# RWKV attention and an MLP mixer on one core: own-step sums from turned products, staggered loads, and a new order of batches zero and one

## The chip, the cores and the metric

The kernel runs on one core of a Trainium2 chip. The metric is the device time of one execution in microseconds (us).

## The reference

Inputs in f32: r, k, v of shape (4, 8, 768, 48), that is batch, head, step, dimension; w and u of shape (8, 48); four weight matrices of the mixer. The attention is a recurrence over the 768 steps, with a decay w and a bonus u for the step's own key:

```python
for t in range(S):
    kt, vt, rt = (k[:, :, t], v[:, :, t], r[:, :, t])
    cur = np.einsum('bhd,bhe->bhde', u[None] * kt, vt)
    y[:, :, t] = np.einsum('bhd,bhde->bhe', rt, state + cur)
    state = w[None, :, :, None] * state + np.einsum('bhd,bhe->bhde', kt, vt)
```

Its output, as x of shape (4, 768, 384), goes through a mixer, first over the steps (tokens), then over the 384 channels:

```python
h = np.maximum(xt @ w_tok1, 0.0) @ w_tok2      # xt: x with steps last
u = x + h.transpose(0, 2, 1)
h2 = np.maximum(u @ w_ch1, 0.0) @ w_ch2
return u + h2
```

Here w_tok1 is 768x256, w_tok2 256x768, w_ch1 384x1536, w_ch2 1536x384.

## The kernel before

**Units.** A batch's 768 steps are cut into 6 chunks of 128 (T), so there are 24 units (b, c). In a unit the recurrence becomes matrix products over 128 steps: k is multiplied by a decay that grows with the step (`wn`) and r by one that shrinks (`wp`), so that scores of decayed k and r, masked to earlier steps, carry the decay between two steps. A state of 4 head pairs goes from unit to unit and is rescaled every third one (`wGm`).

**Stages of a unit.** `stage_p` (L266) makes the decayed k (`kp`) and, in batches 1 to 3, the decayed r (`rp`) and `ku` = k times u, all on POOL but for some `kp` in batch 0. `stage_a` (L288) turns both with transposes on TensorE (PE), copies them out of PSUM as `rk` on ScalarE (ACT), and makes a bf16 copy `vb` of v. `stage_b` (L325) makes the scores `at_ps` on PE and masks them on VectorE (DVE) into `AT`, two instructions of 512 columns. `stage_c` (L351) makes y on PE from the state and from `AT` times v, adds the unit to the state, and on DVE adds the own-step part `yd` into `x_b`.

**The own step.** The step's own term needs, for each step and head, the sum over d of r*u*k, called `adg`. In batches 1 to 3 DVE multiplies `ku` by r (`rku`) and reduces it. In batch 0 POOL makes `m` = k*r, PE turns it in f32, ACT copies it out, and PE multiplies it by `u_blk`, a block matrix of u by head (`ad_ps`). In both, POOL then multiplies v by `adg` into `yd` (`own_step`, L321). In batch 0 r is turned undecayed in f32 (`trr`), from padded tiles (`rpads`), and multiplied after the turn by a turned decay `wpT`.

**Mixer.** `token_mix` (L399) has three parts: `hidden` (token matmuls and relu), `back` (second matmul and the sum `u_sb`) and the turn of `u_sb` into `uT`: on PE for batch 0 (`turn`), by DMA transposes for the others. The channel mixer is `up` (L442: a tile of 128 of the 1536 hidden channels in `z_ps`, relu on ACT into `zr`; 12 tiles for each half `sg` of a batch) and `down` (L453: 12 matmuls for a chunk's output, then the sum `osb` on DVE and a store).

**Order.** A wrapper (`InOrder`) keeps every engine's instructions in the order in which the program issues them. Batch 0 runs in nine slots (L483), in each of which `slot` calls stage_c, b, a and p of four successive units. `keep_warm` puts idle matmuls between. Then the token mixing of batch 0, the first ups with three turns between them, and lists of ups and downs into which `merge` (L520) puts slots of the later batches at given times on a cost scale (an up 0.5, a down 2.0, a slot 1.4).

**Loads.** SP's queue issues the loads of k, r, v, unit by unit (`load_unit`, L82), 192 KB each. POOL's queue issues the weights, which are cast to bf16 on the way: wtok1 in slot 4, wtok2 in slot 5, the first half of wch1 in slot 6, its second half and wch2 in slot 7 (`WEIGHTS_AT`, L247). The first load of batch 1 waits for x_b of the last unit of batch 0 (`after[1, 0] = done[0, C - 1]`, L508), and with it all loads behind it.

All instructions are recorded through the wrapper's line 68, so the profile's rows are told apart by tile names.

Of the kernel before, what the change touches and what calls it, by code (L numbers as in the profile page):

```python
# [11 lines left out]
f32 = mybir.dt.float32  # L12
# [10 lines left out]
def kernel(  # L23
# [51 lines left out]

    loaded = {}
# [3 lines left out]
    rpads = [const.tile([128, H, P], f32, name=f"rpad{c}") for c in range(C)]  # L80

    def load_unit(b, c):  # L82
        tiles = []
        for nm, src in (("kt", k), ("rt", r), ("vt", v)):
            if b == 0 and nm == "rt":
                t = rpads[c]
                dst = t[:, :, 0:D]
            else:
                t = lpool.tile([128, dm], f32, name=nm)
                dst = h3(t)  # L90
            ins = sp.dma_start(dst, src[b, :, ts(c, T), :].rearrange("h s d -> s h d"))
            if (b, c) in after and nm == "kt":
                tc.add_manual_dep(ins.ins, after[b, c].ins.name,
                                  mybir.DependencyInfo(mybir.DependencyClass.Sync,
                                                       mybir.DependencyReason.DATA),
                                  reason="weights first")
            tiles.append(t)
        loaded[b, c] = tiles

    u_bc = const.tile([128, dm], f32, name="u_bc")
    ud = const.tile([128, 3], f32, name="ud")
    w_row = const.tile([1, dm], f32, name="w_row")
    u_row = const.tile([1, dm], f32, name="u_row")
    w_pairs = const.tile([HP, 2, P], f32, name="w_pairs")
    u_rows = const.tile([3, 128], f32, name="u_rows")
    ones = const.tile([1, 128], f32, name="ones")
    act.dma_start(w_row, w.rearrange("h d -> (h d)").unsqueeze(0))  # L110
    dve.memset(w_pairs, 1.0)
    dve.memset(ones, 1.0)
    act.dma_start(w_pairs[:, :, 0:D], w.rearrange("(a q) d -> a q d", q=2))
    act.preload_act_table_set("natural_log_exp_and_others")
    load_unit(0, 0)
    load_unit(0, 1)
    act.dma_start(u_rows, u.rearrange("h d -> (h d)").rearrange("(j p) -> j p", p=128))
    act.dma_start(u_row, u.rearrange("h d -> (h d)").unsqueeze(0))
# [13 lines left out]
    iota_i = const.tile([128, 2 * G], i32, name="iota_i")  # L132
    for g in range(G):
        pool.iota(iota_i[:, g:g + 1], pattern=[[0, 1]], base=g * T - MID, channel_multiplier=1)
        pool.iota(iota_i[:, G + g:G + g + 1], pattern=[[0, 1]], base=MID - 1 - g * T,
                  channel_multiplier=-1)
    iota = const.tile([128, 2 * G], f32, name="iota")
    dve.tensor_copy(iota, iota_i)
    steps_i = const.tile([128, G * T], i32, name="steps_i")
    pool.iota(steps_i, pattern=[[1, G * T]], base=-MID, channel_multiplier=0)  # L140
    steps = const.tile([128, G * T], f32, name="steps")
    dve.tensor_copy(steps, steps_i)
# [4 lines left out]
    for t in rpads[:2]:  # L147
        dve.memset(t[:, :, D:P], 0.0)
# [7 lines left out]
    heads = const.tile([128, 3, H], f32, name="heads")  # L156
    pool.memset(heads, 1.0)
    pool.affine_select(out=heads, in_=heads, compare_op=ALU.is_ge, fill=0.0, base=0,
                       pattern=[[128, 3], [-D, H]], channel_multiplier=1)
    pool.affine_select(out=heads, in_=heads, compare_op=ALU.is_ge, fill=0.0, base=D - 1,  # L160
                       pattern=[[-128, 3], [D, H]], channel_multiplier=-1)

    NB = 3
    rps = []; kps = []; S0s = []
    for i in range(NB):
        kp_i = const.tile([128, H, P], bf16, name=f"kp{i}")
        dve.memset(kp_i, 0.0)
        kps.append(kp_i)

    keep_warm(WARM[0] - 6)  # L170
    w_bc = psM.tile([128, dm], f32, name="w_bc", tag="m")
    pe.matmul(w_bc, ones, w_row, start=True, stop=True)
    wd = psM.tile([128, HP], f32, name="wd", tag="m")
    pe.transpose(wd, w_pairs.rearrange("a q d -> a (q d)"), ident_f[0:HP, 0:HP])
    ud_ps = psM.tile([128, 3], f32, name="ud_ps", tag="m")
    pe.transpose(ud_ps, u_rows, ident_f[0:3, 0:3])
    keep_warm(3)
    lnw = const.tile([128, dm], f32, name="lnw")
    act.activation(lnw, w_bc, Ln)
    wn = const.tile([128, G, dm], f32, name="wn")  # L180
    wp = const.tile([128, G, dm], f32, name="wp")
    lnwd = const.tile([128, HP], f32, name="lnwd")
    wpT = const.tile([128, G, HP, T], f32, name="wpT")

    def decay_k(g):
        act.activation(wn[:, g, :], lnw, Exp, scale=iota[:, G + g:G + g + 1])

    def decay_r(g):
        act.activation(wp[:, g, :], lnw, Exp, scale=iota[:, g:g + 1])

    def decay_rT(g):
        if g == 0:
            for a in range(HP):
                act.activation(wpT[:, g, a, :], steps[:, ts(g, T)], Exp, scale=lnwd[:, a:a + 1])
        else:
            act.activation(wpT[:, g], powers[g - 1], Exp)

    powers = [const.tile([128, HP, T], f32, name=f"powers{g}") for g in range(1, G)]

    def exponents(g):  # L200
        pool.tensor_mul(powers[g - 1], steps[:, ts(g, T)].unsqueeze(1).to_broadcast([128, HP, T]),
                        lnwd.unsqueeze(2).to_broadcast([128, HP, T]))

    decay_k(0)
    act.activation(lnwd, wd, Ln)
    act.copy(ud, ud_ps)
    wG = const.tile([128, HP], f32, name="wG")
    decay_rT(0)
    u_blk = const.tile([128, 3, H], f32, name="u_blk")


    for i in range(2):
        S_i = const.tile([128, HP, 2, D], bf16, name=f"S0_{i}")
        S0s.append(S_i)
    bm = const.tile([128, HP, 2, D], f32, name="bm")
    wGm = const.tile([128, HP, 2, D], f32, name="wGm")


    dve.memset(bm, 0.0)
    for q in range(2):  # L220
        dve.memset(bm[q * P:q * P + D, :, q, :], 1.0)
    for t in rpads[2:]:
        dve.memset(t[:, :, D:P], 0.0)
    for t in S0s:
        dve.memset(t, 0.0)

    def constants_1():
        pool.tensor_mul(u_blk, heads, ud.unsqueeze(2).to_broadcast([128, 3, H]))

    def constants_2():  # L230
        act.activation(wG, lnwd, Exp, scale=float(G * T))
        pool.tensor_mul(wGm, bm, wG.unsqueeze(2).unsqueeze(3).to_broadcast([128, HP, 2, D]))

    def constants_3():

        for i in range(NB):
            rp_i = const.tile([128, H, P], bf16, name=f"rp{i}")
            dve.memset(rp_i, 0.0)
            rps.append(rp_i)

# [4 lines left out]
    wch2 = wts.tile([128, NJ, dm], bf16, name="wch2")  # L245

    WEIGHTS_AT = {4: (0,), 5: (1,), 6: (2,), 7: (3, 4)}  # L247

    def load_weights(which):
        half = ds(0, dch // 2), ds(dch // 2, dch // 2)  # L250
        parts = [(wtok1, moe_w_tok1), (wtok2, moe_w_tok2), (wch1[0], moe_w_ch1[:, half[0]]),
                 (wch1[1], moe_w_ch1[:, half[1]]), (wch2, moe_w_ch2)]
        for i in which:
            t, src = parts[i]
            pool.dma_start(t, src.rearrange("(c p) k -> p c k", p=128))
# [3 lines left out]

    live = {}  # L260
    kv = [None]
    count = [0]

    BY_POOL = (3, 5)

    def stage_p(b, c):  # L266

        g = c % G
        kt, rt, vt = loaded.pop((b, c))
        i = count[0] % NB  # L270
        count[0] += 1
        kp = kps[i]
        vb = apool.tile([128, dm], bf16, name="vb", bufs=4)
        L = live[b, c] = dict(kp=kp, vb=vb, rt=rt, vt=vt)
        (dve if b == 0 and c not in BY_POOL else pool).tensor_mul(kp[:, :, 0:D], h3(kt), h3(wn[:, g, :]))
        if b == 0:
            L["m"] = apool.tile([128, dm], f32, name="m", bufs=2)
            pool.tensor_mul(h3(L["m"]), h3(kt), rt[:, :, 0:D])
        if b > 0:
            L["rp"] = rps[i]  # L280
            pool.tensor_mul(L["rp"][:, :, 0:D], h3(rt), h3(wp[:, g, :]))
            L["ku"] = apool.tile([128, dm], f32, name="ku", bufs=2)
            pool.tensor_mul(L["ku"], kt, u_bc)

    def pair(t, a):
        return t[:, 2 * a:2 * a + 2, :].rearrange("p q d -> p (q d)")

    def stage_a(b, c):  # L288

        L = live[b, c]  # L290
        rk = L["rk"] = apool.tile([128, 2, HP, T], bf16, name="rk")
        if b == 0:

            trk = psM.tile([128, HP, T], bf16, name="trk", tag="m")
            trr = psM.tile([128, HP, T], f32, name="trr", tag="m")
            for a in range(HP):
                pe.transpose(trk[:, a, :], pair(L["kp"], a), ident)
            act.copy(rk[:, 0], trk)
            for a in range(HP):
                pe.transpose(trr[:, a, :], pair(L["rt"], a), ident_f)  # L300
            dve.tensor_mul(rk[:, 1], trr, wpT[:, c % G])
            mT_ps = psM.tile([128, 3, T], f32, name="mT_ps", tag="m")
            for j in range(3):
                pe.transpose(mT_ps[:, j, :], L["m"][:, ts(j, 128)], ident_f)
# [302 lines left out]
```

## Time and profile before

| | |
|---|---|
| median of 3 runs | 185.45 us (185.41 to 185.52) |
| profiled execution | 184.74 us |
| its span | 182.8 us |
| TensorE clock granted | 1.00 |
| DMA | 24.05 MB, mean 132 GB/s |
| instructions: PE / DVE / ACT / POOL | 1507 / 194 / 219 / 113 |

The span runs from the first to the last recorded instruction of the profiled execution. A row of a group gives what is written from what (`out<-in`), shapes, count, busy time, the mean of one in nanoseconds, and the idle time of the engine just before, with the releaser. Rows of a timeline give start and length in us. Matmuls are pipelined: the mean of one is longer than the time from one to the next.

### The profile page before, as it was taken

What the parts mean: (1) busy time and instruction counts of PE and PEld (TensorE: products, weight loads), DVE (VectorE), ACT (ScalarE), POOL (GpSimd) and SP (SyncE); (2) the same over time, 40 slices, a digit from 0 to 9 for tenths busy, and PEclk for the clock granted to TensorE, in tenths of its full rate; (3) what the DMA queues carried; (4) which work ended last, traced back from release to release, by engine and by line L of the source; (5) the groups of instructions that cost most, each with busy time, mean ns of one, the idle gap of its engine ahead of it and who ended that gap; (6) DMA issues with size and microseconds to landing.
All of it is one profiled execution on the core that took longest, in us unless ns stands there. A gap on an engine that the chain in (4) does not pass through costs nothing.

```text
span 182.8 us, 4000 instructions
## 1 busy us (share of the span) xinstructions
PE 166.5 (91%) x1507; PEld 107.7 (59%) x1507; DVE 105.2 (58%) x194; ACT 100.1 (55%) x219; POOL 94.3 (52%) x113
## 2 busy tenths in 40 slices
PE   6999888894997997898999998999999999999992
PEld 2578675462664665556666665756665565666660
DVE  7385877620498999856659868996531061121121
ACT  2777465585867553506949747564545344445500
POOL 5767796004999999925499997981100000000000
PEclk9999999999999999999999999999999999999999
DMA  6999799999999999334799999633001034211212
GB/s 112 182 179 173 139 113 184 190 184 206 183 195 189 192 198 224 108 66 110 127 217 191 184 213 203 131 64 108 24 24 65 20 93 82 87 43 46 83 47 86
DMA packets 89272, 24.05 MB, mean 132 GB/s; under 512 B 82849, under 2 KB 89254, under 8 KB 89254
## 3 DMA queue, kind: packets, MB, share of 16 engines
q1 hardware_dynamic: 85824, 20.65, 62.4%
q0 software_dynamic: 3408, 3.15, 11.5%
q8 instruction: 12, 0.20, 0.5%
q14 instruction: 6, 0.05, 0.1%
q10 hardware_dynamic: 22, 0.01, 0.0%
HBM read 20.45 MB, written 4.72 MB: 138 GB/s over the span
## 4 chain that ended last, share of the span: by engine, by line
PE 53%; POOL 14%; DMA 13%; SPq 7%; DVE 6%; issue 3%; ACT 2%; POOLq 0%; DVEq 0%; ACTq 0%
PE h_ps L68 25%; PE z_ps L68 18%; DMA rt<-in_r_dram 7%; SPq L68 7%; POOL rp L68 4%; DMA rpad<-in_r_dram 3%; POOL yd L68 3%; POOL kp L68 3%; POOL ku L68 3%; PE tr_ps L68 3%; DMA kt<-in_k_dram 2%; PE hT_ps L68 2%; PE y_ps L68 2%; DVE AT L68 2%; PE at_ps L68 2%
## 5 line engine op out<-in xcount | busy, mean ns | idle before, releaser
L68 ACT ACTIVATE zr<-z_ps 128x384 bf16<-128x384 f32 x96 | 43.9, 496 | 31.1 <-PE z_ps L68 31.1
L68 PE MATMUL z_ps<-uT,wch 128*128 128x384 bf16 x288 | 52.1, 326 | 1.7 <-DVE osb L68 0.7
L68 PE MATMUL h_ps<-wch,zr 128*128 128x384 bf16 x288 | 50.4, 326 | 0.3 <-ACT zr L68 0.2
L68 DVE TENSOR_TENSOR osb<-u_sb,h_ps 128x384 f32<-128x384 bf16 x24 | 13.3, 553 | 46.0 <-PE h_ps L68 43.8
L68 PEld LDWEIGHTS <-zr 128*128 128x128 bf16 x288 | 28.0, 98 | 19.1 <-issue 1.1
L68 PEld LDWEIGHTS <-wch 128*128 128x128 bf16 x288 | 27.3, 98 | 19.5 <-issue 3.5
L68 POOL TENSOR_TENSOR kp<-kt,wn 128x384 bf16<-128x384 f32 x20 | 22.9, 1146 | 19.2 <-PE z_ps L68 10.9
L68 DVE TENSOR_TENSOR AT<-at_ps,mask 128x512 bf16<-128x512 f32 x48 | 30.7, 681 | 1.4 <-PE at_ps L68 1.4
L68 ACT COPY rk<-tr_ps 128x1024 bf16<-128x1024 bf16 x18 | 18.2, 1012 | 18.3 <-PE tr_ps L68 17.4
L68 POOL TENSOR_TENSOR yd<-vb,adg 128x384 f32<-128x384 bf16 x24 | 20.0, 834 | 7.3 <-DVE adg L68 6.7
L68 DVE TENSOR_TENSOR rku<-ku,rt 128x384 f32<-128x384 f32 x18 | 16.1, 892 | 9.7 <-POOL ku L68 9.6
L68 POOL TENSOR_TENSOR rp<-rt,wp 128x384 bf16<-128x384 f32 x18 | 18.6, 1031 | 2.1 <-DMA rt<-in_r_dram 2.1
L68 POOL TENSOR_TENSOR ku<-kt,u_bc 128x384 f32<-128x384 f32 x18 | 19.3, 1072 | 0.0
L68 DVE TENSOR_TENSOR x_b<-y_ps,yd 128x384 bf16<-128x384 f32 x24 | 13.3, 554 | 9.2 <-PE y_ps L68 5.4
L68 PEld LDWEIGHTS <-rk 48*128 48x128 bf16 (+1 forms) x272 | 11.3, 95 | 5.3 <-issue 2.0
L68 ACT CAST S<-kv_ps 48x192 bf16<-48x192 f32 x32 | 9.9, 310 | 7.4 <-PE kv_ps L68 7.1
L68 PEld LDWEIGHTS <-kp 128*128 128x128 bf16 x176 | 11.2, 101 | 4.4 <-POOL kp L68 0.9
L68 PEld LDWEIGHTS <-wtok 128*128 128x128 bf16 x96 | 9.1, 98 | 7.6 <-issue 2.4
L68 DVE TENSOR_TENSOR u_sb<-x_b,hT_ps 128x384 bf16<-128x384 bf16 x24 | 11.8, 548 | 2.3 <-PE hT_ps L68 2.3
L68 ACT CAST vb<-vt 128x384 bf16<-128x384 f32 x24 | 12.4, 515 | 0.0
L68 PE MATMUL tr_ps<-ident,rp 128*128 128x128 bf16 x72 | 7.0, 220 | 4.8 <-POOL rp L68 4.7
L68 DVE TENSOR_REDUCE adg<-rku 128x8 f32<-128x384 f32 x18 | 10.0, 553 | 0.8
(78 smaller groups left out, 166.4 us busy)
## 6 DMA issues: line engine op xcount, KB each, us to landing
kt<-in_k_dram SPq DMA_DIRECT2D x24, 192.0 KB, 4.4
vt<-in_v_dram SPq DMA_DIRECT2D x24, 192.0 KB, 4.6
out_dram<-osb SPq DMA_DIRECT2D x24, 192.0 KB, 1.9
rt<-in_r_dram SPq DMA_DIRECT2D x18, 192.0 KB, 4.6
rpad<-in_r_dram SPq DMA_DIRECT2D x6, 192.0 KB, 4.7
wch<-in_moe_w_ch_dram POOLq DMA_DIRECT2D x2, 576.0 KB, 7.8
wch<-in_moe_w_ch_dram POOLq DMA_DIRECT2D x1, 1152.0 KB, 15.7
wtok<-in_moe_w_tok_dram POOLq DMA_DIRECT2D x2, 384.0 KB, 5.3
```

Of the source, the lines that this page charges most:

```text
L68: return lambda *args, **kw: tc.keep_in_program_order(f(*args, **kw))
```

## The change

- The own-step sum is made in all batches on PE: k and r are both decayed and turned as in the later batches before (`kr`, one tile for both, turned into `krT`), DVE multiplies the two turned halves (`own`), and four small matmuls with `wu_blk` (w times u, in a block of two columns for a head pair) give `ad_ps`. At a step's own place the two decays leave one factor 1/w, which w in `wu_blk` takes back. `ku`, `rku`, its reduction, `m`, `trr`, `wpT`, `u_blk`, `heads` and their constants are gone.
- `vb` is used for the matmuls only; `yd` is made from v itself.
- The mask is applied by one instruction of 1024 columns; `at_ps` is one tile of two banks.
- Loads are staggered: k of a unit, r of the one before, v of the one before that. Batch 1's first load waits for the landing of the first half of wch1.
- Weights are asked for one at a time behind POOL's `yd` of units 2, 3 and 4 of batch 0, and the last three together behind `yd` of unit 5. wch2 comes in two halves.
- Batch 0 is an order written out by hand, with 10 idle matmuls at the start (behind `w_bc`) and two or three a unit. All six turns of its `u_sb` come before the first up.
- Batch 0's 24 ups run in a row, then its six downs with batch 1's slots between them; batch 1's `uT` is turned by PE. A slot is now stage_p, stage_c, then `whole` (own, scores, v), stage_a and stage_e.
- One relu in four of the ups of batches 0 to 2 is made by DVE, one of two in each token mixing; `osb` has 4 buffers.

The core of the diff (`by_dma` is never true for the 24 units, `WEIGHTS_IN` is empty):

```diff
+    queue = []
+    for lo, hi in ((0, C), (C, B * C)):
+        q = [(n - lag, x) for n in range(lo, hi + 2) for lag, x in ((0, "k"), (1, "r"), (2, "v"))]
+        queue += [(n // C, x, n % C) for n, x in q if lo <= n < hi]
...
+            landed = pool.dma_start(t, src.rearrange("(c p) k -> p c k", p=128))
+            if i == 2:
+                after[1, "k", 0] = landed
...
+    def stage_a(b, c):
...
+        for i in range(2):
             for a in range(HP):
+                pe.transpose(kr_ps[:, i, a, :], pair(L["kr"][:, i], a), ident)
+        act.copy(krT, kr_ps)
+
+    def stage_o(b, c):
+        L = live[b, c]
+        L["own"] = apool.tile([128, HP, T], bf16, name="own", bufs=2)
+        dve.tensor_mul(L["own"], L["kT"], L["rT"])
...
+        AT = L["AT"] = apool.tile([128, 2 * HP, T], bf16, name="AT")
+        dve.tensor_mul(AT, at_ps.rearrange("p q a t -> p (q a) t"),
+                       mask.unsqueeze(1).to_broadcast([128, 2 * HP, T]))
+
+    def stage_e(b, c):
+        L = live[b, c]
+        ad_ps = psM.tile([128, HP, 2], f32, name="ad_ps", tag="m")
+        for a in range(HP):
+            pe.matmul(ad_ps[:, a, :], L["own"][:, a, :], wu_blk[:, a, :], start=True, stop=True)
+        L["adg"] = apool.tile([128, H], f32, name="adg")
+        act.copy(L["adg"], ad_ps.rearrange("p a q -> p (a q)"))
...
+    STEPS = dict(p=stage_p, a=stage_a, o=stage_o, b=stage_b, c=stage_c, e=stage_e, v=v_copy)
...
+    play(0, "p0 p1 a0 x2")
+    constants_0()
+    constants_1()
+    play(0, "b0 v0 o0 x2 e0")
+    play(0, "a1")
+    decay(0, 2)
+    decay(1, 2)
+    play(0, "p2 b1 v1 o1 e1 c0 x2 p3 a2")
+    constants_2()
+    play(0, "b2 v2 o2 e2 c1 x3 w0 p4 a3 b3 v3 o3 e3 c2 w1 x3 p5 a4 b4 v4 o4 e4 c3 w2 x3 a5 b5 v5 o5 e5 c4 w3 w4 w5")
...
+    def whole(b, c):
+        stage_o(b, c)
+        stage_b(b, c)
+        v_copy(b, c)
...
+    STAGES = ((0, stage_p), (3, stage_c), (2, whole), (1, stage_a), (2, stage_e))
...
+    items = ups(0, 0) + u1 + downs(0, 0) + downs(0, 1)
```

In the strings, a letter is a stage and a digit a unit; `x3` is three idle matmuls, `w0` a weight.

More of the change, by code (lines that the diff above doesn't have):

```diff
@@ L78, with load_next @@
     after = {}
[L80 to L93, printed above, removed]
+    queue = []
+    for lo, hi in ((0, C), (C, B * C)):
+        q = [(n - lag, x) for n in range(lo, hi + 2) for lag, x in ((0, "k"), (1, "r"), (2, "v"))]
+        queue += [(n // C, x, n % C) for n, x in q if lo <= n < hi]
+    src = dict(r=r, k=k, v=v)
+    def load_next(n=1):
+        for _ in range(n):
+            b, what, c = queue.pop(0)
+            t = lpool.tile([128, dm], f32, name=what + "t")
+            ins = sp.dma_start(h3(t), src[what][b, :, ts(c, T), :].rearrange("h s d -> s h d"))
+            loaded[b, what, c] = t
+            if (b, what, c) in after:
+                tc.add_manual_dep(ins.ins, after[b, what, c].ins.name,
                                   mybir.DependencyInfo(mybir.DependencyClass.Sync,
@@ L129, in keep_warm @@
             pe.matmul(z_ps, warm[:, 0:128], warm, start=True, stop=True)
[L132 to L137, printed above, removed]
+    iota_i = const.tile([128, 2, G], i32, name="iota_i")
+    pool.iota(iota_i[:, 0], pattern=[[-T, G]], base=MID - 1, channel_multiplier=-1)
+    pool.iota(iota_i[:, 1], pattern=[[T, G]], base=-MID, channel_multiplier=1)
+    iota = const.tile([128, 2, G], f32, name="iota")
     dve.tensor_copy(iota, iota_i)
[L139 to L142, printed above, removed]
     ident_f = const.tile([128, 128], f32, name="ident_f")
@@ L154 @@
     )
[L156 to L168, printed above, removed]
@@ L170 @@
-    keep_warm(WARM[0] - 6)
+    NK = 4
+    krs = [const.tile([128, 2, H, P], bf16, name=f"kr{i}") for i in range(NK)]
+    S0s = [const.tile([128, HP, 2, D], bf16, name=f"S0_{i}") for i in range(2)]
+    wGm = const.tile([128, HP, 2, D], f32, name="wGm")
+    wu_blk = const.tile([128, HP, 2], bf16, name="wu_blk")
+    for t in krs:
+        dve.memset(t[:, :, :, D:P], 0.0)
     w_bc = psM.tile([128, dm], f32, name="w_bc", tag="m")
     pe.matmul(w_bc, ones, w_row, start=True, stop=True)
-    wd = psM.tile([128, HP], f32, name="wd", tag="m")
@@ L181 @@
-    wp = const.tile([128, G, dm], f32, name="wp")
+    wkr = const.tile([128, 2, G, dm], f32, name="wkr")
     lnwd = const.tile([128, HP], f32, name="lnwd")
[L183 to L206, printed above, removed]
-    wG = const.tile([128, HP], f32, name="wG")
[L208 to L214, printed above, removed]
@@ L234, in constants_3, with decay, constants_0 @@
[L234 to L239, printed above, removed]
+    def decay(i, g):
+        act.activation(wkr[:, i, g, :], lnw, Exp, scale=iota[:, i, g:g + 1])
+    decay(0, 0)
+    decay(1, 0)
+    decay(0, 1)
+    decay(1, 1)
+    wud = const.tile([128, 2, HP], f32, name="wud")
+    wG = const.tile([128, HP], f32, name="wG")
+    def constants_0():
+        act.copy(wud, wu_ps)
+        act.activation(lnwd, wu_ps[:, 0, :], Ln)
+        act.activation(wG, lnwd, Exp, scale=float(G * T))
@@ L266, in stage_p @@
[L266 to L283, printed above, removed]
@@ L285, in pair, with stage_p @@
     def pair(t, a):
         return t[:, 2 * a:2 * a + 2, :].rearrange("p q d -> p (q d)")
+    def stage_p(b, c):
+        n = b * C + c
+        kr = krs[n % NK]
+        live[b, c] = dict(kr=kr, kp=kr[:, 0])
+        for i, what, by_dve in ((0, "k", K_BY_DVE), (1, "r", R_BY_DVE)):
+            if i == 1:
+                load_weights(*WEIGHTS_IN.get(n, ()))
+            (dve if n in by_dve else pool).tensor_mul(
+                kr[:, i, :, 0:D], h3(loaded.pop((b, what, c))), h3(wkr[:, i, c % G, :]))
@@ L288, in stage_a @@
     def stage_a(b, c):
         L = live[b, c]
[L291 to L295, printed above, removed]
-            for a in range(HP):
[L297 to L304, printed above, removed]
-            L["mT"] = apool.tile([128, 3, T], f32, name="mT", bufs=2)
-            act.copy(L["mT"], mT_ps)
-            act.copy(L["vb"], L["vt"])
-            return
@@ L309, in stage_a @@
-        tr_ps = psM.tile([128, 2, HP, T], bf16, name="tr_ps", tag="m")
-        for j, src in ((0, L["kp"]), (1, L["rp"])):
-            for a in range(HP):
-                pe.transpose(tr_ps[:, j, a, :], pair(src, a), ident)
-        act.copy(rk, tr_ps)
-        act.copy(L["vb"], L["vt"])
-        rku = apool.tile([128, dm], f32, name="rku", bufs=2)
-        dve.tensor_mul(rku, L["ku"], L["rt"])
-        L["adg"] = apool.tile([128, H], f32, name="adg")
-        dve.tensor_reduce(L["adg"], h3(rku), axis=mybir.AxisListType.X, op=ALU.add)
@@ L321, in own_step @@
-    def own_step(L):
-        L["yd"] = apool.tile([128, dm], f32, name="yd")
-        pool.tensor_mul(h3(L["yd"]), h3(L["vb"]), L["adg"].unsqueeze(2).to_broadcast([128, H, D]))
+        krT = apool.tile([128, 2, HP, T], bf16, name="krT")
+        L["kT"], L["rT"] = krT[:, 0], krT[:, 1]
+        if by_dma(b, c):
+            sp.dma_start_transpose(krT.rearrange("p x a t -> p (x a) t"),
+                                   L["kr"].rearrange("p x h d -> p (x h d)"))
+            return
+        kr_ps = psM.tile([128, 2, HP, T], bf16, name="kr_ps", tag="m")
@@ new lines, in stage_a, with v_copy @@
+        for i in range(2):
+            for a in range(HP):
+                pe.transpose(kr_ps[:, i, a, :], pair(L["kr"][:, i], a), ident)
[4 more added lines that the diff above has]
+        dve.tensor_mul(L["own"], L["kT"], L["rT"])
+    def v_copy(b, c):
+        L = live[b, c]
+        L["vb"] = apool.tile([128, dm], bf16, name="vb", bufs=4)
+        act.copy(L["vb"], loaded[b, "v", c])
@@ L325, in stage_b @@
     def stage_b(b, c):
         L = live[b, c]
-        rk = L["rk"]
-        if b > 0:
-            own_step(L)
-        at_ps = [psA.tile([128, HP, T], f32, name=f"at_ps{q}", tag=f"at{q}") for q in range(2)]
+        kT, rT = L["kT"], L["rT"]
+        at_ps = psA.tile([128, 2, HP, T], f32, name="at_ps", tag="at")
         for a in range(HP):
@@ L334, in stage_b @@
                 rows = slice(q * P, q * P + D)
-                pe.matmul(at_ps[q][:, a, :], rk[rows, 0, a, :], rk[rows, 1, a, :], start=True, stop=True)
-        L["AT"] = []
-        for q in range(2):
-            AT = apool.tile([128, HP, T], bf16, name=f"AT{q}")
-            dve.tensor_mul(AT, at_ps[q], mask.unsqueeze(1).to_broadcast([128, HP, T]))
-            L["AT"].append(AT)
-        if b == 0:
-            ad_ps = psM.tile([128, H], f32, name="ad_ps", tag="m")
-            for j in range(3):
-                pe.matmul(ad_ps, L["mT"][:, j, :], u_blk[:, j, :], start=(j == 0), stop=(j == 2))
-            L["adg"] = apool.tile([128, H], f32, name="adg")
-            act.copy(L["adg"], ad_ps)
+                pe.matmul(at_ps[:, q, a, :], kT[rows, a, :], rT[rows, a, :], start=True, stop=True)
+        AT = L["AT"] = apool.tile([128, 2 * HP, T], bf16, name="AT")
+        dve.tensor_mul(AT, at_ps.rearrange("p q a t -> p (q a) t"),
+                       mask.unsqueeze(1).to_broadcast([128, 2 * HP, T]))
+    def stage_e(b, c):
+        L = live[b, c]
+        ad_ps = psM.tile([128, HP, 2], f32, name="ad_ps", tag="m")
[3 more added lines that the diff above has]
+        act.copy(L["adg"], ad_ps.rearrange("p a q -> p (a q)"))
+        L["yd"] = apool.tile([128, dm], f32, name="yd")
+        pool.tensor_mul(h3(L["yd"]), h3(loaded.pop((b, "v", c))), L["adg"].unsqueeze(2).to_broadcast([128, H, D]))
     state = {}
@@ L471, in slot, with load_units @@
                 f(*units[s - lag])
-    ahead = [2]
-    def load_next(n=1):
-        for _ in range(n):
-            if ahead[0] < len(units):
-                load_unit(*units[ahead[0]])
-                ahead[0] += 1
-    load_next(4)
-    hid, bk, tn = token_mix(0, by_pe=True)
-    for s in range(C + 3):
-        slot(s, 0, C)
-        if s < C:
-            keep_warm(WARM[1 if s < 4 else 2])
-        if s < 2:
-            decay_k(s + 1)
-            exponents(s + 1)
-        if s == 0:
-            constants_1()
-        if s == 3:
-            constants_2()
-        if 0 < s < 3:
-            decay_rT(s)
-        if s == 8:
-            constants_3()
-        if 4 < s < 8:
-            decay_r(s - 5)
-        load_weights(WEIGHTS_AT.get(s, ()))
-        if s == C + 2:
-            ub_ps = psM.tile([128, dm], f32, name="ub_ps", tag="m")
-            pe.matmul(ub_ps, ones, u_row, start=True, stop=True)
-            act.copy(u_bc, ub_ps)
-        if s == C + 1:
-            for f in hid[:3]:
-                f()
-    after[1, 0] = done[0, C - 1]
-    for f in hid[3:]:
-        f()
-    for f in (bk[0], bk[1], bk[2], tn[0], tn[1], tn[2], bk[3], bk[4], bk[5]):
-        f()
-    for c in range(3):
-        up(0, 0, 2 * c)
-        up(0, 0, 2 * c + 1)
-        tn[3 + c]()
+    def load_units(n):
+        load_until(*units[min(n, B * C - 1)])
+    for f in tn[3:]:
+        f()
     def merge(items, events):
@@ L553, in woven, with part, go @@
         return out
[L555 to L556 removed]
+    load_units(C + 2)
     u1 = ups(0, 1)
[L560 to L564 removed]
+    items = ups(0, 0) + u1 + downs(0, 0) + downs(0, 1)
+    def part(t, cost, f, *args):
+        return (t, cost, lambda: f(*args))
+    def go(fs):
+        for f in fs:
+            f()
+    times = (9.0, 12.0, 15.0, 18.0, 21.0, 24.0, 27.0, 30.0, 33.0)
+    t14 = times[-1]
+    events = [(t, SLOT if j < 6 else 1.4 - .4 * (j - 5),
+               lambda s=6 + j: (slot(s, C, 2 * C), load_units(s + 3))) for j, t in enumerate(times)]
+    hid, bk, tn = token_mix(1, by_pe=True)
+    events += [part(t14 - 6.0 + 3.0 * j, 0, stage_p, 2, j) for j in range(3)]
+    events += [part(t14 + 0.5, 0.5, stage_a, 2, 0), part(t14 + 1.6, 2.0, go, hid),
+               part(t14 + 4.2, 1.3, go, bk[:3]), part(t14 + 5.4, 0.5, go, bk[3:5]),
+               part(t14 + 5.5, 0.2, go, tn[:3] + bk[5:]),
+               part(t14 + 5.6, 0.5, whole, 2, 0), part(t14 + 5.8, 0.5, stage_a, 2, 1), part(t14 + 8, 0.2, stage_e, 2, 0)]
+    late = tn[3:]
+    merge(items, events)
     for b in range(1, B):
@@ L573 @@
             total = span + 4.0 + SLOT * len(at)
[L574 to L575 removed]
+            events += mixing(b + 1, total - 9.0, total - 4.5, total - 2.0)
+        if b == 1:
+            events += [(0.4 + i, 0.2, f) for i, f in enumerate(late)]
         merge(items, events)
```

121 lines of the change are left out of this document (61 added, 60 removed).

## The prediction

> **What bounds the kernel now.** I read the page's head first, then busy time by stage.
>
> ```profile
> span 182.8 us, 4000 instructions
> ...
> PE 166.5 (91%) x1507; PEld 107.7 (59%) x1507; DVE 105.2 (58%) x194; ACT 100.1 (55%) x219; POOL 94.3 (52%) x113
> ...
> PE 53%; POOL 14%; DMA 13%; SPq 7%; DVE 6%; issue 3%; ACT 2%; POOLq 0%; DVEq 0%; ACTq 0%
> ```
> ```profile
> 52.00:73.00 21.00, 18.02 (x236) 12.46 (x234) 19.88 (x33) 11.79 (x24) 21.00 (x22) 1.00 1.19 200
> 73.00:179.00 106.00, 103.44 (x878) 65.34 (x878) 54.40 (x97) 55.19 (x116) 42.13 (x44) 1.00 0.48 102
> ```
> Columns of the second fence: length, then busy PE, PEld, DVE, ACT, POOL, then clock. From 73 us on PE is 98% busy and sets the end. From 52 to 73 POOL is busy without a break. The waits of PE from 46 us on, and two pieces of the chain, say what that costs:
>
> ```profile
> PE tr_ps L68 <- POOL rp L68: 4.7, 6, 2.5
> PE tr_ps L68 <- POOL kp L68: 0.8, 1, 0.8
> ```
> ```profile
> 32.14 12.55 DMA rt<-in_r_dram
> ...
> 173.39 5.86 PE h_ps L68 x36
> 179.28 0.55 DVE osb L68
> ```
> PE stands 5.5 us for POOL's rp and kp. The last 36 matmuls take 5.86, so one of 384 columns is issued each 0.163, and 3.6 us lie between the last one (179.2) and the end of the span.
>
> Now PE's order in time, first in batch 0, then around the first hidden-layer matmul of the channel mixing (z_ps):
>
> ```profile
> 5.77 2.31 PE L68 MATMUL idle_ps<-warm 128*128 128x512 bf16 x5
> ...
> 15.68 0.59 PE L68 MATMUL idle_ps<-warm 128*128 128x512 bf16 x2
> 16.11 0.33 PE L68 MATMUL y_ps<-S,rk 128*128 128x96 bf16 x4
> ...
> 25.02 0.40 PE L68 MATMUL at_ps<-rk 48*128 48x128 bf16 x8 [0.25 <-DVE rk L68]
> ...
> 28.51 0.40 PE L68 MATMUL at_ps<-rk 48*128 48x128 bf16 x8 [0.25 <-DVE rk L68]
> ```
> ```profile
> 31.81 1.15 PE L68 MATMUL h_ps<-x_b,wtok 128*128 128x384 bf16 x6
> ...
> 36.66 1.14 PE L68 MATMUL z_ps<-uT,wch 128*128 128x384 bf16 x6
> ...
> 45.88 0.40 PE L68 MATMUL tr_ps<-ident,rp 128*128 128x128 bf16 x4 [2.48 <-POOL rp L68]
> ...
> 49.09 0.40 PE L68 MATMUL tr_ps<-ident,kp 128*128 128x128 bf16 x4
> 49.32 0.39 PE L68 MATMUL tr_ps<-ident,rp 128*128 128x128 bf16 x4
> 49.54 0.65 PE L68 MATMUL z_ps<-uT,wch 128*128 128x384 bf16 x3
> ...
> 59.37 0.33 PE L68 MATMUL y_ps<-S,rk 128*128 128x96 bf16 x4
> 59.54 0.33 PE L68 MATMUL kv_ps<-vb,kp 128*128 128x96 bf16 x4
> 59.71 0.36 PE L68 MATMUL y_ps<-vb,AT 128*128 128x48 bf16 x8
> 60.01 0.40 PE L68 MATMUL at_ps<-rk 48*128 48x128 bf16 x8
> 60.34 0.40 PE L68 MATMUL tr_ps<-ident,kp 128*128 128x128 bf16 x4
> ```
> A unit of batch 0 takes 3.5 us (25.02 to 28.51), its scores (at_ps) of unit 5 start at 28.5, and z_ps starts at 36.7. So the time is: start of z_ps, plus PE's work from there, plus what PE stands still in it, plus 3.6. I work out each for the new kernel.
>
> **Batch 0: the new round.** PE runs its instructions in the order written. The new order for one unit is: turn k and r (8 transposes); scores; the four sums `ad_ps`, whose weights are the product `own`; stage_c of the unit before; two or three idle matmuls; then the next unit's transposes. The product stands on VectorE behind the score mask, so PE, waiting at the sums, holds up everything behind them: stage_c, the idle matmuls, the next transposes. In the kernel before, the sums in PE took a tile that ScalarE had long made. The links:
>
> ```profile
> 5.03 0.49 ACT L68 ACTIVATE lnw<-w_bc 128x384 f32<-128x384 f32 x1 [1.59 <-PE w_bc L68]
> ```
> ```profile
> 49.79 1.01 ACT L68 COPY rk<-tr_ps 128x1024 bf16<-128x1024 bf16 x1
> ```
> ```profile
> 46.81 0.56 DVE L68 TENSOR_TENSOR rku<-ku,rt 128x384 f32<-128x384 f32 x1 [9.12 <-POOL ku L68]
> 49.19 1.29 DVE L68 TENSOR_TENSOR AT<-at_ps,mask 128x512 bf16<-128x512 f32 x2 [1.16 <-PE at_ps L68]
> ```
> ```profile
> L68 DVE TENSOR_TENSOR AT<-at_ps,mask 128x512 bf16<-128x512 f32 x48 | 30.7, 681 | 1.4 <-PE at_ps L68 1.4
> ...
> L68 POOL TENSOR_TENSOR yd<-vb,adg 128x384 f32<-128x384 bf16 x24 | 20.0, 834 | 7.3 <-DVE adg L68 6.7
> L68 DVE TENSOR_TENSOR rku<-ku,rt 128x384 f32<-128x384 f32 x18 | 16.1, 892 | 9.7 <-POOL ku L68 9.6
> ...
> L68 POOL TENSOR_TENSOR ku<-kt,u_bc 128x384 f32<-128x384 f32 x18 | 19.3, 1072 | 0.0
> L68 DVE TENSOR_TENSOR x_b<-y_ps,yd 128x384 bf16<-128x384 f32 x24 | 13.3, 554 | 9.2 <-PE y_ps L68 5.4
> ```
> - Transposes 0.62 (49.09 to 49.71); copy out 1.01; scores 0.40. Each change of engine 0.08 (49.71 to 49.79), four of them.
> - Mask, now one instruction of 1024 columns: 512 take 681 ns and 384 take 554, so 1024 take 1.19 (bound above: the pair's 1.29).
> - `own`, 512 columns, 16-bit throughout, not in the trace. Above: 0.68 (AT), or 1.2 with POOL in the way as the longer rku are; below: half the columns' time of a 384 one, some 0.23. I take 0.45, the middle, because POOL is idle when it runs in batch 0. Mask and product overlap by 0.07 (1.29 against twice 0.681).
> - Four sums: 0.15, by the 0.30 of eight 48-column matmuls (59.71 to 60.01).
> - stage_c 0.64 (59.37 to 60.01); three idle matmuls 0.64 (two take 0.43, 15.68 to 16.11).
>
> Sum 0.62 + 1.01 + 0.40 + 0.32 + 1.57 + 0.15 + 0.64 + 0.64 = 5.35 us a unit, against 3.5. Loads, staggered or not, can't shorten it: the 18 of batch 0 are issued at the same pace as now. They hide under the round. The cheaper constants and gone f32 transposes lie off it too.
>
> Start: ScalarE's logarithm ends the wait for w at 5.0. Ten idle matmuls now come behind it at 0.46 (five in 2.31), about 4.6, then two small turns (0.4), transposes, copy and hops (1.8): scores of unit 0 at 11.7, the last idle ones being faster. Unit 0 to 1 has no stage_c and its two idle matmuls lie under the mask: 4.1. Then 5.0 (two idle ones, no y from S), 5.35, 5.35, 5.5 (one 384-column matmul for the state more): scores of unit 5 at 37.0. From there 2.1 to the sums, 2.3 for sums, stage_c, six token-mixing matmuls and unit 5's own y, 0.6 for x_b, 0.5 for the last matmuls: 42.5, where the kernel before had 33.0 (31.81 + 1.15).
>
> ```profile
> 36.21 1.48 DVE L68 TENSOR_TENSOR u_sb<-x_b,hT_ps 128x384 bf16<-128x384 bf16 x3 [0.76 <-PE hT_ps L68]
> ```
> From 33.0 to z_ps it took 3.7. Now turns 3 to 5, which wait for the last u_sb (37.7, that is 4.7 behind), stand ahead of z_ps: 5.0. **z_ps starts at 47.5, 10.8 later.** How the weights are asked for can't move this: x_b isn't there earlier.
>
> **The rest, PE's work.** 648 matmuls of 384 columns: 105.5. A unit now: 0.64 + 0.33 scores (60.01 to 60.34) + 0.45 transposes (49.09 to 49.54) + 0.15 sums = 1.57; 18 units, less 1.0 for first and last ones, plus 0.5 for states: 27.8. Eighteen turns at 0.056: 1.0. Together 134.3. By the same count the kernel before has 131.1, so 36.7 + 131.1 + 3.6 = 171.4, and PE stood 11.4 us.
>
> **The rest, standing.** POOL loses ku (1.07 of some 4.0 us a unit), so 5.5 us of waits for rp and kp go, since the batch's attention now runs one unit for each 1.95 us of down matmuls. What is late next is again `own`. In a slot, x_b waits for y_ps: from stage_c's start 0.8, to 1.36; `own` behind it, 0.45 to 0.55, ends near 1.85; the sums can go at 1.9, while PE is there at 1.43 (0.64 + 0.33 + 0.45). PE stands 0.4 to 0.5, say 0.42, in 17 slots: 7.1. Two first slots without enough work between them: mask and product must end before y: 1.4. Batch 1's token mixing is now turned by PE, waiting for h1r and six u_sb (half a us each) ahead of its first z_ps: 2.0 beyond the work put in between. Batches 2 and 3: 0.8. Sum 11.3. The relu of every fourth hidden tile on VectorE, and the larger osb pool, lie under PE's 0.49 a tile (three matmuls of 0.163): nothing.
>
> Span 47.5 + 134.3 + 3.6 + 11.3 = 196.7. The profiled execution before took 184.74 for a span of 182.8, and its median is 0.71 higher (185.45): 196.7 + 1.94 + 0.71 = **199.4**.
>
> A row and a rule that speak against the change: rku, with both inputs in SBUF, takes 0.56 alone and 0.89 on average, in the stretch where POOL is full. The Trainium skill, "SBUF — State Buffer", section "SBUF: two separate sides", says that a VectorE instruction with two SBUF inputs and a GpSimd one that reads SBUF lock each other out for a whole instruction; the row agrees. `own` is such an instruction, as the masks are not. By that rule (POOL busy some 60%, half an instruction of 1.07 lost each time) `own` would take 0.3 more in 17 slots: about 204.
>
> **Batch 1's loads.** SP's first load of batch 1 now waits for weight 2's landing; behind it stand all later loads.
>
> ```profile
> DMA to landing us min/median/max: 7.2/8.5/15.7
> ```
> POOL asks for it behind yd of unit 4: sums at 33.6, some 0.5 of sums and copy, 0.83: 35.0; landed at 42.2 to 43.5. The third load, r of unit 6, is issued 0.8 later and may take the 12.55 of the chain row among the other weights: 56; POOL's product 57. PE wants it after 22 ups at 58.2. Hidden, with about a microsecond to spare.
>
> **Rivals.**
> - *PE doesn't stand at the sums* (the product is ready before PE is there). Each round loses 0.08 + 1.57 + 0.08 = 1.73, six times 10.4, and the slots their 7.1 less a tenth or two: 199.4 − 17 = 182, faster. It decides from 14 us on. For it: POOL's relief. Against: the product follows the mask on VectorE. 0.04.
> - *Clock.* PE is under half busy in the new round. At half clock its 2.45 us a round (0.62 + 0.40 + 0.15 + 0.64 + 0.64) double: 5.5 rounds, 13.5 us, 213. Against: after 2.48 idle the transposes at 45.88 take 0.40 as at 49.09; the round's longest stand is 1.7. The Trainium skill, "TensorE: Matmul & The Clock Gate", part 1, lets the clock fall after an idle window of about 3.4 us; by that rule no fall here, and the trace agrees. 0.06.
> - *Batch 1's loads come late*: they pass the spare microsecond by 4: 203.5. 0.15.
> - *Own steps quick in the slots*: standing falls to 5: 193. 0.10.
>
> **The numbers.** My forecast 0.65, and the rivals as given. Low end: `own` at 0.23, part of the idle matmuls hidden (2.5 off) and standing at 5: 190.5. High end: `own` at 0.9 in batch 0 (2.7) and loads late: 206.5. Faster or slower means by more than 0.2%, what a measurement here can tell: faster 0.04, same 0.01, slower 0.95.
>
> **What would show it.** Right: scores in batch 0 5 to 5.5 us apart; PE waiting for own, in batch 0 some 1.7 each and 0.4 in the slots; first z_ps near 47.5; no more waits for rp. Wrong: scores under 4 us apart, z_ps before 42, a granted clock below 1, or PE waiting for a load between 55 and 80.

## The result, and the profile after

The changed kernel takes 207.7 us (median of 4, 205.6 to 208.8) against 185.4: ratio 1.117, 95% interval 1.108 to 1.126. It is slower, as forecast, but by 22 us where 14 were forecast, and just above the range (206.5). The page is that of the slowest of the four executions (208.8), as is that of e6 below (184.3).

```profile
span 207.1 us, 4037 instructions
...
PE 174.3 (84%) x1573; PEld 108.4 (52%) x1573; DVE 97.0 (47%) x167; ACT 96.7 (47%) x209; POOL 68.8 (33%) x84
...
PEclk9995555557999969999999999999999999999999
```

The last row is the clock granted to TensorE in 40 slices of 5.2 us. It was 9 throughout before; now it is halved for six slices from the fourth on, and dips once more around 75 us. PE's order in time in batch 0 and up to the first z_ps:

```profile
10.29 0.40 PE L68 MATMUL at_ps<-krT 48*128 48x128 bf16 x8 [0.67 <-ACT krT L68]
...
14.24 0.40 PE L68 MATMUL at_ps<-krT 48*128 48x128 bf16 x8 [1.10 <-ACT krT L68]
17.06 0.27 PE L68 MATMUL ad_ps<-wu_blk,own 128*128 128x2 bf16 x4 [2.42 <-DVE own L68]
...
20.80 0.61 PE L68 MATMUL at_ps<-krT 48*128 48x128 bf16 x8 [1.10 <-ACT krT L68]
23.06 0.27 PE L68 MATMUL ad_ps<-wu_blk,own 128*128 128x2 bf16 x4 [1.66 <-DVE own L68]
...
24.14 1.46 PE L68 MATMUL idle_ps<-warm 128*128 128x512 bf16 x3
25.38 1.06 PE L68 MATMUL kr_ps<-ident,kr 128*128 128x128 bf16 x8
27.55 0.61 PE L68 MATMUL at_ps<-krT 48*128 48x128 bf16 x8 [1.10 <-ACT krT L68]
...
41.38 0.61 PE L68 MATMUL at_ps<-krT 48*128 48x128 bf16 x8 [1.10 <-ACT krT L68]
...
54.37 10.89 PE L68 MATMUL z_ps<-uT,wch 128*128 128x384 bf16 x66
```

From unit 2 on each round has the forecast stands: 1.66 at the sums for mask and product, 1.10 at the scores for the copy out. At unit 1's sums PE stands longer, 2.42, because the product takes 1.18 there, beside a product of POOL's, and 0.42 in the other rounds. But the links of PE itself have doubled: eight transposes take 1.06 in place of 0.62, three idle matmuls 1.25 from start to start (24.14 to 25.38) in place of 0.64. Scores are 6.75 apart (20.80 to 27.55) and z_ps starts at 54.4. PE's waits over the whole run, then over the part from 50 us on, each answer's first rows:

```profile
PE ad_ps L68 <- DVE own L68: 17.4, 22, 2.4
PE at_ps L68 <- ACT krT L68: 6.2, 6, 1.1
```
```profile
PE ad_ps L68 <- DVE own L68: 7.1, 16, 1.2
PE y_ps L68 <- DVE AT L68: 0.7, 1, 0.7
```

The waits for POOL's rp and kp (5.5 us before) are gone. Waits for own have taken their place: 10.3 us in batch 0 and 7.1 after it.

### The profile page after: what moved, and what is told of

Its sections match the earlier page's. It is cut to its first block, busy times and chain, and to the rows that moved or that the text cites. A ratio compares the mean times of both kernels' runs of the same rounds, so it can differ in the third digit from the quotient of the medians.

```text
span 207.1 us, 4037 instructions
## 1 busy us (share of the span) xinstructions
PE 174.3 (84%) x1573; PEld 108.4 (52%) x1573; DVE 97.0 (47%) x167; ACT 96.7 (47%) x209; POOL 68.8 (33%) x84
## 3 DMA queue, kind: packets, MB, share of 16 engines
q1 hardware_dynamic: 83328, 20.06, 44.9%
q0 software_dynamic: 3424, 3.15, 10.3%
## 4 chain that ended last, share of the span: by engine, by line
PE 66%; DVE 10%; ACT 10%; issue 8%; DMA 4%; POOL 1%; SPq 0%; DVEq 0%; ACTq 0%; POOLq 0%
PE h_ps L68 26%; PE z_ps L68 18%; DVE own L68 5%; ACT krT L68 4%; PE idle_ps L68 4%; PE hT_ps L68 3%; ACT S L68 3%; PE y_ps L68 3%; PE kr_ps L68 3%; PE ad_ps L68 2%; DVE AT L68 2%; PE kv_ps L68 2%; PE at_ps L68 2%; DMA rt<-in_r_dram 2%; DMA uT<-u_sb 1%
## 5 line engine op out<-in xcount | busy, mean ns | idle before, releaser
L68 POOL TENSOR_TENSOR yd<-vt,adg 128x384 f32<-128x384 f32 x24 | 19.9, 828 | 70.6 <-ACT adg L68 65.1
L68 ACT COPY krT<-kr_ps 128x1024 bf16<-128x1024 bf16 x24 | 24.3, 1012 | 22.2 <-PE kr_ps L68 22.0
L68 DVE TENSOR_TENSOR AT<-at_ps,mask 128x1024 bf16<-128x1024 f32 x24 | 29.2, 1218 | 11.1 <-PE at_ps L68 11.0
L68 POOL TENSOR_TENSOR kr<-rt,wkr 128x384 bf16<-128x384 f32 x23 | 23.3, 1012 | 11.8 <-DMA rt<-in_r_dram 11.8
L68 POOL TENSOR_TENSOR kr<-kt,wkr 128x384 bf16<-128x384 f32 x21 | 21.1, 1003 | 5.1 <-ACT wkr L68 5.1
L68 PEld LDWEIGHTS <-kr 128*128 128x128 bf16 x272 | 18.5, 107 | 4.6 <-issue 2.4
L68 DVE TENSOR_SCALAR zr<-z_ps 128x384 bf16<-128x384 f32 x18 | 10.0, 557 | 20.2 <-PE z_ps L68 20.1
L68 PEld LDWEIGHTS <-krT 48*128 48x128 bf16 (+1 forms) x272 | 11.9, 102 | 11.7 <-ACT krT L68 7.9
L68 PE MATMUL kr_ps<-ident,kr 128*128 128x128 bf16 x192 | 16.6, 236 | 0.0
L68 PE MATMUL at_ps<-krT 48*128 48x128 bf16 x192 | 10.4, 233 | 6.2 <-ACT krT L68 6.2
```

The costliest lines, as they stand in the source:

```text
L68: return lambda *args, **kw: tc.keep_in_program_order(f(*args, **kw))
```

## The experiments

Theory A: PE stands at the sums for the product behind the mask; its share of busy time in batch 0 is then so low that its granted clock halves, which lengthens every link of the round. Rivals: the clock is a side effect of a fixed chain; loads or POOL set the pace; the stands are only exchanged for others. Each kernel was timed in three rounds beside the kernel before.

**The clock alone (e1).** Idle matmuls go where PE stands anyway:

```diff
-a3 b3 v3 o3 e3 c2 w1 x3
+a3 x3 b3 v3 o3 x6 e3 c2 w1 x3      (and so for units 1 to 5; in unit 0 six in place of two)
```


> The changed kernel with idle matmuls added where PE stands still in batch 0: three behind each unit's transposes (under the copy out of PSUM) and six between scores and sums (under mask and product). Theory A, the clock: PE is busy too small a share of the round, so its granted clock halves from 15.7 us on and every PE link of the round takes twice as long; filled stands keep the clock at 1.0, scores of batch 0 come 5.2 to 5.5 us apart in place of 6.75, the first z_ps starts near 47 in place of 54.4, and the time falls to 199 to 201. Theory B, the clock is a side effect and the round is a chain of fixed lengths: scores stay 6.7 apart or more, time 207 to 210.

197.9 us, ratio 1.069 (1.066 to 1.072). One window of it (length, then busy time of PE, PEld, DVE, ACT and POOL with the number of instructions in brackets, clock, DMA share, GB/s) and its scores:

```profile
15.70:41.00 25.30, 21.17 (x236) 11.69 (x237) 14.83 (x23) 9.51 (x22) 13.63 (x16) 1.00 0.60 85
```
```profile
19.10 0.40 PE L68 MATMUL at_ps<-krT 48*128 48x128 bf16 x8 [0.46 <-ACT krT L68]
...
24.17 0.40 PE L68 MATMUL at_ps<-krT 48*128 48x128 bf16 x8 [0.46 <-ACT krT L68]
...
29.24 0.40 PE L68 MATMUL at_ps<-krT 48*128 48x128 bf16 x8 [0.46 <-ACT krT L68]
...
34.49 0.40 PE L68 MATMUL at_ps<-krT 48*128 48x128 bf16 x8 [0.46 <-ACT krT L68]
...
44.90 10.89 PE L68 MATMUL z_ps<-uT,wch 128*128 128x384 bf16 x66
```

The same stretch of the changed kernel had:

```profile
15.70:41.00 25.30, 14.92 (x144) 9.87 (x144) 12.30 (x18) 7.50 (x17) 10.64 (x13) 0.50 0.45 67
```

More work in PE, and 9.8 us less time. The clock stays at 1.00, scores are 5.07 apart, z_ps starts 9.5 us earlier. So the clock was a cause and not a side effect; with it held, the kernel takes within 1.5 us what the prediction's sum gave (below).

**Idle matmuls on the chain (e2).** The x2 and x3 of the rounds are left out, nothing put in.

> The changed kernel without the idle matmuls of the rounds of batch 0 (those of the start and of unit 0 stay). Theory A: three of them lie on the chain and take 1.25 us a unit at half clock; PE is even less busy, so the clock still halves; scores 5.4 to 5.6 apart, first z_ps near 49, time 202 to 203. Rival: they lie beside a wait for other engines or hold the clock up, so nothing or less than 1 us is gained (207), or the time grows.

203.3 us, ratio 1.098 (1.094 to 1.102): 4.4 us gained. Scores 5.5 to 5.8 apart, the clock again 0.50 from 20 to 40 us, z_ps at 50.0. The idle matmuls lay on the chain, and three a unit were not enough to hold the clock.

**The product ahead of the mask (e3).**

```diff
-a3 b3 v3 o3 e3 c2
+a3 o3 b3 v3 e3 c2      (and so for every unit of batch 0)
```


> The changed kernel with the product own ahead of the score mask on VectorE in batch 0, so that PE's sums wait for the product alone. Theory A: the stand at the sums falls from 1.66 us by the mask's 1.15; scores 5.6 apart if the clock still halves (first z_ps near 48, time near 201), 4.1 if PE is then busy enough to keep its clock (first z_ps near 41, time near 194). Rival, the round is set by something else (POOL, loads): less than 2 us gained, 206.

192.2 us, ratio 1.039 (1.035 to 1.043), z_ps at 39.9. Better than the better of the two cases, by 2, though the clock was not kept as that case has it: it halved from 15.5 to 25.8 us (0.64 on average between 12 and 25), so scores are 5.4 apart in the middle and 3.6 at the end, where that case put 4.1:

```profile
22.66 0.61 PE L68 MATMUL at_ps<-krT 48*128 48x128 bf16 x8 [1.10 <-ACT krT L68]
...
27.36 0.40 PE L68 MATMUL at_ps<-krT 48*128 48x128 bf16 x8 [1.10 <-ACT krT L68]
...
30.99 0.40 PE L68 MATMUL at_ps<-krT 48*128 48x128 bf16 x8 [1.10 <-ACT krT L68]
```

The order of two instructions on VectorE was worth 15 us: 1.2 a round directly, some 7 in six rounds. The rest is put down to the clock, which was at half for 10 us here and for 38 in the changed kernel; that split was not measured apart.

**The sums a slot later, batches 1 to 3 (e4).**

```diff
-STAGES = ((0, stage_p), (3, stage_c), (2, whole), (1, stage_a), (2, stage_e))
+STAGES = ((3, stage_e), (3, stage_c), (2, whole), (1, stage_a), (0, stage_p))
```


> The changed kernel with the sums of a unit moved to the next slot in batches 1 to 3, ahead of stage_c, and stage_p moved behind the others; batch 0 unchanged. Standing theory: PE's 7.1 us of waits for own after 50 us fall below 1, time near 201. Rival, the wait moves on (yd comes later, so x_b and the product behind it on VectorE, and PE waits there): 206 to 208.

199.8 us, ratio 1.083 (1.077 to 1.088). stage_p moves behind the others with it, so the two moves are not told apart. The first four of its waits from 50 us on:

```profile
PE z_ps L68 <- ACT krT L68: 1.3, 2, 1.0
PE y_ps L68 <- DVE AT L68: 1.1, 2, 0.7
PE ad_ps L68 <- DVE u_sb L68: 0.9, 1, 0.9
PE z_ps L68 <- DVE u_sb L68: 0.6, 1, 0.6
```

Waits for own are gone from this part, 7.1 us before. From the first z_ps (52.8) to the end of the span (197.6) it takes 144.8, against 152.7; 1.7 of the difference is the second clock dip, which it does not have. Some 3 us of small waits have come up (5.3 in all, against 2.1 beside those for own before).

**Turning ahead (e5), and both (e6).** In batch 0 the product goes ahead of the mask, and the next unit's transposes ahead of the present unit's sums:

```diff
-a3 b3 v3 o3 e3 c2 w1 x3 p5
+o3 b3 v3 a4 p5 e3 c2 w1 x2
```

e6 has this, e4's slots, and turns 3 to 5 of batch 0 between the first ups.

> The changed kernel with batch 0 alone rewritten: product ahead of the mask, and the next unit's transposes on PE ahead of the present unit's sums, stage_p a unit earlier; two idle matmuls a unit. Theory A: copy out, mask and product then run beside each other, the round falls to the pace of the loads (3.3 to 3.7 us), PE is busy enough to keep its clock at 1.0, unit 5's scores near 29, first z_ps near 38, and the time is that of the changed kernel less some 16 us: 190 to 192. Rival: PE is still busy under half, the clock halves and scores come 4.5 us or more apart (z_ps after 42, time 195 or more); or batch 1's loads, bound to the weights, hold PE up between 45 and 70.

> The order of batch 0 of e5, the sums a slot later as in e4, and turns 3 to 5 of batch 0 between the first ups as in the kernel before. If the two stands and the clock are all of the loss, their gains add: 207.7 less 16 less 6 to 7 less 1: 183 to 185, level with the kernel before or just ahead. Rival: the next limit (loads of batch 1, VectorE) takes part of it back: 187 to 190.

e5: 189.4 us, ratio 1.021 (1.014 to 1.028), scores of unit 5 at 25.5, z_ps at 35.0, some 19 us earlier than in the changed kernel. The clock did not keep 1.00 as expected: it halves from 16.8 to 23.6 us, behind a stand of 2.56 at unit 2's sums, and once more from 54.3 to 57.7. e6: 181.9 us, ratio 0.981 (0.977 to 0.986), faster than both kernels. The gains add up but for 1 to 2 us: 207.7 less 18.3 (e5), less 7.9 (e4), less about 1 for the turns (an estimate) is 180.5. Where batch 0 still loses shows in e6, on VectorE (first two rows) and PE:

```profile
16.61 1.81 DVE L68 COPY wGm<-wG 48x192 f32<-48x192 f32 x2
18.45 0.43 DVE L68 TENSOR_TENSOR own<-krT 128x512 bf16<-128x512 bf16 x1
```
```profile
18.94 0.25 PE L68 MATMUL ad_ps<-wu_blk,own 128*128 128x2 bf16 x4 [2.56 <-DVE own L68]
```

The constant wGm stands ahead of unit 2's product, PE stands 2.56, and the clock halves from 19.4 to 22.8 us (0.72 on average between 20 and 25).

**The staggered loads (e7).** e6 with the loads in the old order.

```diff
-for lag, x in ((0, "k"), (1, "r"), (2, "v"))]
+for lag, x in ((0, "k"), (0, "r"), (0, "v"))]
```


> e6 with the loads in the order of the kernel before (k, r, v of a unit together). If the staggering matters only where loads set the pace: with batch 0 near the loads' pace a unit's r and k come one or two loads later at most, 0 to 1.5 us slower than e6. Rival, loads hide: within 0.3 us of e6.

182.1 us, ratio 0.983 (0.978 to 0.988): no difference from e6 beyond the scatter. The staggering hides even where batch 0 is fast.

**The kernel before without idle matmuls (e8).** `WARM = (10, 2, 1)` becomes `(10, 0, 0)`.

> The kernel before without the idle matmuls of batch 0's slots (those of the start stay). It measures what PE share the clock needs: PE is then busy some 65 to 70% there, against 47% in the changed kernel. If a share somewhere above 47% is enough, the clock stays at 1.0 and the time within 0.5 us of 185.0 (PE isn't the limit there); if the clock needs more, it halves and the time grows by 2 to 5 us.

185.5 us, ratio 1.000 (0.997 to 1.003). Its batch 0:

```profile
10.00:28.00 18.00, 14.46 (x194) 12.58 (x194) 12.76 (x23) 11.90 (x33) 15.12 (x17) 1.00 1.15 155
```

PE is busy 80% there (more than the 65 to 70 I had put), and the clock holds. In batch 0 the kernel before did not need them. Later, where nothing was changed, e8's clock did fall: it halves from 46.9 to 50.3 us, behind a stand of 2.45 us for rp. It is the very stand of 2.48 that the prediction leans on (45.88 there).

**The filled version (e9), and earlier weights (e10).** e9 is e6 with wGm made later and `x3` in the stands of batch 0. e10 is e6 with the first four weights asked for a unit earlier.

> e6 with the constant wGm made on VectorE behind unit 1's own part (in e6 it stood ahead of unit 2's product for 2.2 us, and PE stood 2.6 there) and three idle matmuls in the stands of batch 0. Clock theory: the clock of e6, 0.72 between 20 and 25 us, stays at 1.0, unit 3's scores come 2 to 3 us earlier, unit 5's by 1 to 2 (the loads then set the pace), and the time falls by 1 to 2 us to 180 to 181. Rival: loads set unit 5's scores already, so nothing is gained (181.5 to 182.5).

> e6 with every weight asked for one unit earlier, so batch 1's first load, bound to the third weight, starts some 2.5 us earlier. If the weights' place hides, as the prediction had it, the time stays within 0.7 us of e6 (181.2 to 182.6). Rival: batch 1's loads set the pace of its attention, and it gains 1 to 2.5 us (179.5 to 181); or the weights push back batch 0's last loads, and it loses 1 or more.

e9: 181.3 us, ratio 0.977 (0.971 to 0.982), the lowest median of all. The clock is 1.00 in every window up to 70 us, unit 5's scores start at 24.7 and z_ps at 32.7 (33.9 in e6). The gain over e6 is 0.7, not told from scatter: e9's executions took 180.3 to 183.4, e6's 181.5 to 184.3. e10: 181.6, ratio 0.980 (0.977 to 0.983): as e6. A unit earlier or later, when the weights are asked for does not show.

## Why the prediction was right or wrong

The sign, and the place and kind of the loss, were right; the size failed in one step, the clock: the sum took every link of PE in the round at full clock, and they ran at half.

- *The round.* 5.35 at full clock was forecast; with the clock held (e1) it is 5.07. The product takes 0.42 (forecast 0.45), the mask 1.22 (1.19), the copy 1.01. Unit 0's scores start at 10.3, not 11.7. In e1 z_ps starts at 44.9 (forecast 47.5), the span is 195.9 (196.7) and the time 197.9 (199.4). e1 is thus near the kernel whose time I predicted; that it fits within 1.5 us is in part luck, since z_ps came 2.6 early and the rest took 1.8 more.
- *The clock: the step that failed.* The rival "Clock" had a chance of 0.06 and a price of 13.5. The price was of the right order (the changed kernel takes 9.8 more than e1); the chance was not. I reasoned that a stand has to be long: 2.48 us idle before had left the clock alone, the longest stand forecast was 1.7, and the Trainium skill, "TensorE: Matmul & The Clock Gate", part 1, names an idle window of about 3.4 us. The trace differs from that rule, and decides. In the traces here the clock changes only a whole number of 3.41 us apart (in the changed kernel at 15.35, 49.48, 73.37 and 76.78), so it is granted in steps. The steps ahead of the two falls:

```profile
11.93:15.34 3.41, 1.12 (x20) 0.78 (x20) 1.09 (x3) 2.34 (x5) 1.40 (x2) 1.00 1.03 199
69.96:73.36 3.40, 1.89 (x34) 1.35 (x32) 2.52 (x4) 2.87 (x7) 2.66 (x3) 1.00 1.03 220
```

  PE was busy 33% of the first and 56% of the second: neither idle. That 2.48 us had left the clock alone was luck. In the profiled execution before, a step ends inside that stand and splits it; in e8 one step holds most of it, and the next is at half. The step of the kernel before that holds the longer part, then those two of e8:

```profile
44.35:47.76 3.41, 1.88 (x15) 1.24 (x16) 0.85 (x2) 1.45 (x3) 2.88 (x3) 1.00 1.18 189
```
```profile
43.47:46.88 3.41, 1.33 (x11) 0.93 (x12) 0.40 (x1) 0.90 (x1) 2.25 (x3) 1.00 1.25 203
46.90:50.29 3.39, 3.39 (x20) 1.52 (x18) 0.70 (x3) 2.64 (x7) 3.39 (x4) 0.50 0.86 141
```

  PE is busy 55% of the one and 39% of the other. Of the 13 executions of the kernel before that were timed beside e5 to e8, six have a mean clock of 0.987 to 0.991, so about one such step at half (half of 3.41 in 183 us is 0.009); where it lay in them is not on record. I had written "PE is under half busy in the new round" into the rival, a share that lost the clock in every step that shows it (last section), and still weighed it by its longest gap. What sums up from it: scores 0 to 5 took 31.1 us against 25.3 forecast, and the way from there to z_ps 13.0 against 10.5, as the clock stays halved until 49.5. Less the 1.4 by which unit 0's scores were early, z_ps is 6.9 late.
- *The first slots.* 1.4 us of standing were forecast and 1.5 measured (0.69 for AT, 0.82 for own), but not that the clock answers. The next down's 12 matmuls take 3.4 us from start to start (72.94 to the y at 76.34) in place of 1.95: 1.5 more, and some tenths behind it:

```profile
72.94 3.61 PE L68 MATMUL h_ps<-wch,zr 128*128 128x384 bf16 x12
76.34 0.53 PE L68 MATMUL y_ps<-S,krT 128*128 128x96 bf16 x4
```

- *Standing in the slots.* 7.1 us were forecast in 17 slots, 0.42 each, and 7.1 measured in 16 waits. That the sums agree is in part luck: 0.8 of it is that of the first slots, eight waits are of 0.2 or less, and the other eight of 0.3 to 1.2. e4 gains 6.2 there beside the clock dip, with some 3 us of other waits come up, so they were lost about in full. Here the rule of the Trainium skill, "SBUF — State Buffer", section "SBUF: two separate sides", on VectorE and GpSimd locking each other out agrees with the trace: own takes 0.42 in the 17 units where POOL makes no product beside it, 0.45 to 1.18 in the other seven, and 0.517 on average over its 24. Its price of 4 us more was too high: in batches 1 to 3 own is longer by 1.7 in all.
- *The rest.* From the first z_ps to the end 149.2 were forecast and 151.0 measured in e1, 152.7 in the changed kernel, which has the second dip.
- *POOL's relief* was right (no wait for rp or kp is left) and so was what it is worth: nothing, as long as PE stands at the sums instead. That it pays once PE does not is not shown: e6 and e9 beat the kernel before by 3 to 4 us, but in e9 all of that lies ahead of z_ps (32.7 against 36.7), and from there to the end of the span it takes 145.9 against 146.1.
- *Loads and weights* hide, as put (e7, e10). The rival "batch 1's loads late" did not come about: POOL waited 8.0 us for r of unit 6, had its product at 57.5 (forecast 57), and PE, late by then, wanted it at 65.1 (forecast 58.2). It was close, though: in e1, with the clock held, the product is done at 55.5 and PE wants it at 55.6, where a microsecond to spare was forecast.
- *The range* failed with the clock: its high end held late loads and a slow product, and left the clock out at a chance of 0.06.

What of the change costs how much: the clock about 10 us, 1.7 of it the second dip; the mask ahead of the product and the missing overlap of batch 0 some 8.5 more beside it (e5 gains 18.3 in all; the 8.5 is what is left, and e5 still has a clock dip of its own); the sums within their own slot some 6. The relu on VectorE, the osb pool and the order of ups and downs were not tried apart.

## What to carry to other kernels

When a small matmul is put in PE's queue whose weights another engine has just to make, count what stands behind it in the queue: here four tiny matmuls held up a 5 us round, and moving them behind independent work, or their product ahead of a longer instruction, won it back. Put a stretch's busy share of PE beside its longest gap before trusting the clock: half-busy stretches of a few microseconds lost it here, and idle matmuls held it only where they lay in the stands; on the chain they cost time. Look at more than one execution for it: the same stand kept the clock in one and lost it in another. Add up such fixes in one kernel: the changed kernel was 12% slower than the old one as ordered, and 2% faster once PE no longer waited for the product.

## What the runs showed of the hardware that was not expected

The clock halved without any idle window. It is granted in steps of 3.41 us, which lie differently in each execution, and what counts here is PE's busy share of one step. In the twelve profiled executions, of the kernel before, the changed one and e1 to e10, all 11 steps at full clock with PE busy under half (0.15 to 0.49) were followed by a step at half clock, 4 of the 11 with 0.52 to 0.62, and none of the 546 with 0.63 or more. It came back only behind steps with PE busy over 0.8, counted at half clock. So a stretch near half can go either way by where the steps cut it: the first slots of batch 1 lost the clock in the changed kernel (1.89 of 3.40), and kept it in e1, where the steps that hold them had 2.58 and 2.63 of 3.41. Executions of the changed kernel differ by 1.6%, and their mean clock with them (0.907 to 0.940).

And the two small copies of wGm, 48x192, took 1.81 us in e6, where POOL was busy with products, against 0.52 in the changed kernel, where POOL was idle.
